# Sigmoid attention and a bilinear FFN: x passed through memory in 512-token blocks, twelve plain pairs, w1 and w2 decoded in twelve pieces

## The chip, the core and the metric

The kernel runs on one NeuronCore of a Trainium2 chip. The metric is the device time of one execution in microseconds (us); of several executions the median is taken.

## The reference

Eight batches of twelve heads, 448 tokens, head size 64. Attention has a sigmoid in place of a softmax; its output is the input x of a bilinear feed-forward net on 3584 tokens:

```
scores = q @ k.T / 8 - log(448)
x      = concat_heads(sigmoid(scores) @ v)          # 3584 x 768
out    = ((x @ w1) * (x @ w2)) @ w3 @ w_out         # 768 -> 1024 -> 1024 -> 768
```

All arrays are float32, except that the host hands over w1, w2, w3 and w_out as 64-bit words of float64 values, which the kernel decodes to float32 itself.

## The kernel before

**Precision by splitting.** A float32 operand is split into a high part rounded to float32r and the rest as a low part (`split`, L66 casts, L67 subtracts). A product of two such operands is then three float32r matmuls: high by high, high by low, low by high. "Plain" pairs of heads skip this: their scores (L196) and their products with v (L248) are float32 matmuls.

**Attention in slots.** Two heads make a pair; 8 batches of 6 pairs are 48 pairs. The keys of a pair fall into four chunks (128, 128, 128 and 64 keys, NC = 4); one chunk is a slot, so there are 192. In a slot the program writes the score products (`scores`, or `short_scores` for the 64-key chunk of a split pair, L225), the sigmoids on ScalarE (L180; split pairs take two of them, and VectorE makes the low part al, L217), the decode and split steps that fall due, a dozen products of the filler, and then the av products (L255 or L248) of the slot before. Before the change the first 9 pairs (PLAIN) are plain. `split_pair` makes qs, kh, kl, ks of the next pair: VectorE casts qs and kh and subtracts (L158, L159, L66), POOL makes kl (L67) and ks (L165). After the last chunk, `combine` writes x of the pair as xh and xl into SBUF; two sets of six such tiles (px0, px1) serve even and odd batches.

**The up products as filler.** `up(b)` is a generator of 288 matmuls for one batch: 8 fc by 2 weights by 6 kc by 3, each of 448 columns (L318). Between slots `take` draws 12 of them (`ups`). The up products of batch b - 1 run while batch b is in attention, from its slot 2 on; those of batch 7 run after attention. Each fc ends with a copy of the w1 product (a_sb, L326), a multiply (g, L329) and a store to memory at once (L330).

**Decoding weights.** A job loads words (L74), takes the magnitude on ScalarE (`magnitude`, Abs, L79), does six VectorE operations (`decode`, L86, L91, L94, L98, L99, L102), and is split into w high (ScalarE, L66) and w low (VectorE, L67) some slots later. w1 and w2 take 16 jobs of 768 elements a partition, the first eight from slot 1 on, three slots apart, the others from slot 25 on; w3 takes 16 jobs of 512 during attention, which go back to memory; w_out is decoded after attention in 16 halves.

**After attention** come the last up products, w3 times w_out (L508), and the output products of 512 columns (L524), in seven blocks of TB = 512 tokens, for which g is loaded from memory.

**Order.** Until slot PLAIN x NC - 2 the order of TensorE, SP (which issues the DMAs), ScalarE and POOL is as written; after it that of TensorE and SP only, and a scheduler orders the others. VectorE's order is the scheduler's from the start. At that slot the pool pp of early words gives its memory to the tiles of the split pairs (pf).

Of the kernel before, what the change touches and what calls it, by code (L numbers as in the profile page):

```python
# [25 lines left out]
def sigmoid_attention_bilinear_ffn(  # L26
# [16 lines left out]
    nc = tc.nc  # L43
# [12 lines left out]
    PLAIN = 9  # L56
# [5 lines left out]
    w3_dram = dram.tile([NF, P, NF, P], F32, name="w3_dram")  # L62
    g_dram = dram.tile([NF, P, NT], F32, name="g_dram")
# [5 lines left out]
    def load_words(src, pool=None):  # L69
        if pool is None:  # L70
            raw = pd.tile([P, NK, P, 2], U32, name="raw", bufs=1)[:, :src.shape[1]]
# [5 lines left out]
    def magnitude(raw, early=False):  # L77
        f = (pp if early else pd).tile([P, *raw.shape[1:-1]], F32, name="f", bufs=3 if early else 2)
        nc.scalar.activation(f, raw[..., 1].bitcast(F32), AF.Abs, scale=HW_SCALE)  # L79
        return f  # L80
# [26 lines left out]
    px1 = phase_x.enter_context(tc.tile_pool(name="px1", bufs=NK, side="left"))  # L107
    pm = phase_x.enter_context(tc.tile_pool(name="pm", bufs=2, side="left"))
# [3 lines left out]
    px = (px0, px1)  # L112
# [147 lines left out]
    def combine(b, accs):  # L260
        xh = px[b % 2].tile([P, S], F32R, name="xh")
        xl = px[b % 2].tile([P, S], F32R, name="xl")
        if len(accs) == 1:
            split(xh, xl, accs[0][:, :S], nc.scalar.copy, nc.vector)
            return xh, xl
        t = pm.tile([P, S], F32, name="t", bufs=1)
        add_halves(t, [acc[:, :S] for acc in accs])
        split(xh, xl, t, nc.scalar.copy, nc.vector)
        return xh, xl
# [19 lines left out]
    def load_job(i):  # L289
        _, _, cs, src = jobs[i]  # L290
        raws[i] = load_words(src[:, cs], pp) if i < EARLY else load_words(src[:, cs])

    def decode_job(i):
        if i + 2 < EARLY:
            load_job(i + 2)
        for k in (i, i + 1):
            if k not in fs and k in raws:
                fs[k] = magnitude(raws[k], k < EARLY)
        f = decode(raws.pop(i), fs[i])
        if EARLY <= i + 1 < len(starts):  # L300
            load_job(i + 1)
        n, at, cs, _ = jobs[i]
        if n == 3:
            nc.sync.dma_start(out=w3_dram[at, :, cs], in_=f)

    def split_job(i):
        n, at, cs, _ = jobs[i]
        split(wh[n][:, at, cs], wl[n][:, at, cs], fs.pop(i), nc.scalar.copy, nc.vector)

    def up(b, xs, banks):  # L310

        for fc in range(NF):
            for n in (1, 2):
                acc = ps.tile([P, 512], F32, name="up", tag=next(banks), bufs=2)
                for kc in range(NK):
                    xh, xl = xs[kc]
                    for m, (w, x) in enumerate(((wh[n], xh), (wh[n], xl), (wl[n], xh))):
                        nc.tensor.matmul(  # L318
                            acc[:, :S], w[:, fc, kc], x,
                            start=(kc == 0 and m == 0), stop=(kc == NK - 1 and m == 2),  # L320
                        )
                        if (kc, m) != (NK - 1, 2):
                            yield
                if n == 1:
                    a_sb = pm.tile([P, S], F32, name="a_sb", bufs=1)
                    nc.scalar.copy(out=a_sb, in_=acc[:, :S])  # L326
                    yield
            g = pm.tile([P, S], F32, name="g", bufs=1)
# [234 lines left out]
```

## Time and profile before

| what | value |
|---|---|
| median of 3 runs | 1082.26 us (1080.23 to 1083.45) |
| profiled execution, its time | 1081.56 us |
| its span, first to last instruction | 1079.5 us |
| granted TensorE clock, mean | 0.998 |
| busy share of the span | TensorE 99%, VectorE 66%, ScalarE 52%, POOL 18% |
| DMA | 129.15 MB, mean 120 GB/s |

PE is TensorE, PEld its weight loads, DVE is VectorE, ACT ScalarE, SPq the queue of the engine that issues DMAs. A matmul's listed duration (some 370 ns at 448 columns) holds its way through the array, in which the next one already runs; what a product costs the engine is the distance between two starts. A bracket behind a row of the timeline says how long the engine was idle before it and what ended that.

### The profile page before, as it was taken

Reading aid. Unit: us, or ns where it says so; the run is one execution under the profiler, and the core shown is the slowest. Engines: PE = TensorE matmul, PEld = TensorE weight load, DVE = VectorE, ACT = ScalarE, POOL = GpSimd, SP = SyncE. Lnnn points to the kernel's source line nnn. Section 1 sums busy time; section 2 is a strip of 40 time slices with the busy share of each in tenths; the row PEclk is TensorE's granted clock in tenths of the full one; section 3 lists DMA queues with packets and bytes.
Section 4 is the critical chain, followed back from the end, with each engine's and each line's share of the span. In section 5 each row is a group of like instructions: output and inputs, shape, how many; then the busy total and the mean of one; then the engine's idle time right before and its main releaser. Section 6 shows DMA issues by size and latency. Waiting matters only on the chain.

```text
span 1079.5 us, 14155 instructions
## 1 busy us (share of the span) xinstructions
PE 1067.9 (99%) x5094; PEld 915.1 (85%) x5094; DVE 714.1 (66%) x1074; ACT 563.4 (52%) x789; POOL 190.1 (18%) x277
## 2 busy tenths in 40 slices
PE   8999899999999999999999999999999999999998
PEld 3256799999999999999999989999999888888886
DVE  5997978888878878888887877649862133223321
ACT  5855666776776677767767766653342011101100
POOL 0002432232233323232332224200000000000000
PEclk9999999999999999999999999999999999999999
DMA  8755434443543535344452543225471032233211
GB/s 257 231 166 146 103 95 122 124 132 104 140 118 103 141 107 135 112 131 115 116 154 79 135 122 92 68 75 180 137 243 39 20 127 93 84 127 127 88 49 49
DMA packets 100693, 129.15 MB, mean 120 GB/s; under 512 B 8016, under 2 KB 82960, under 8 KB 100624
## 3 DMA queue, kind: packets, MB, share of 16 engines
q1 hardware_dynamic: 100624, 128.25, 40.6%
q8 instruction: 40, 0.66, 0.3%
q14 instruction: 29, 0.24, 0.1%
HBM read 98.34 MB, written 29.88 MB: 119 GB/s over the span
## 4 chain that ended last, share of the span: by engine, by line
PE 94%; DVE 2%; DMA 1%; ACT 1%; issue 1%; SPq 0%; ACTq 0%
PE up L318 42%; PE up L524 21%; PE av L255 10%; PE sp L199 9%; PE up L508 6%; PE sp L196 2%; PE av L248 2%; PE sp L225 1%; DMA raw<-w 1%; DVE f L102 0%; ACT f L79 0%; DVE w L67 0%; DVE raw L99 0%; DVE f L94 0%; ACT ap L180 0%
## 5 line engine op out<-in xcount | busy, mean ns | idle before, releaser
L318 PE MATMUL up<-xh,w 128*128 128x448 f32 x1536 | 467.2, 368 | 0.0
L318 PEld LDWEIGHTS up<-xh,w 128*128 128x128 f32 x1536 | 288.8, 188 | 31.6 <-issue 5.9
L318 PE MATMUL up<-xl,w 128*128 128x448 f32 x768 | 281.2, 366 | 0.0
L524 PE MATMUL up<-w 128*128 128x512 f32 x1008 | 228.7, 389 | 0.0
L524 PEld LDWEIGHTS up<-w 128*128 128x128 f32 x1008 | 189.2, 188 | 39.2
L180 ACT ACTIVATE ah<-sp,bias 128x896 fp32r<-128x896 f32 x117 | 117.6, 1005 | 114.3 <-PE sp L199 113.5
L217 DVE TENSOR_TENSOR al<-sp,ah 128x896 fp32r<-128x896 f32 x117 | 127.5, 1090 | 50.0 <-ACT sp L180 49.0
L67 POOL TENSOR_TENSOR kl<-kk,kh 128x896 fp32r<-128x896 f32 x39 | 89.5, 2294 | 402.5 <-DVE kh L66 380.3
L318 PEld LDWEIGHTS up<-xl,w 128*128 128x128 f32 x768 | 144.4, 188 | 12.5
L534 DVE COPY o_sb<-up 128x512 f32<-128x512 f32 x42 | 29.0, 691 | 161.0 <-PE up L524 161.0
L66 ACT CAST w<-graw 128x1024 fp32r<-128x1024 f32 x28 | 29.4, 1056 | 175.9 <-PE up L524 170.5
L180 ACT ACTIVATE sp<-sp,bias 128x896 f32<-128x896 f32 x117 | 113.6, 971 | 0.0
L255 PE MATMUL av<-ah,vs 128*128 128x448 f32 x312 | 102.4, 368 | 3.8 <-DVE ah L239 2.7
L255 PE MATMUL av<-al,vs 128*128 128x448 f32 x234 | 86.1, 368 | 0.4 <-DVE al L217 0.4
L199 PE MATMUL sp<-qs,kh 128*128 128x448 f32 x234 | 86.3, 369 | 0.0
L67 POOL TENSOR_TENSOR vs<-vv,vs 128x256 fp32r<-128x256 f32 x78 | 68.2, 885 | 102.8 <-DVE vs L66 95.0
L199 PE MATMUL sp<-qs,kl 128*128 128x448 f32 x234 | 86.3, 369 | 0.0
L239 DVE TENSOR_TENSOR ah<-st,ah 64x448 fp32r<-64x448 f32 x78 | 59.3, 760 | 18.7 <-ACT st L180 16.8
L255 PEld LDWEIGHTS av<-ah,vs 128*128 128x128 f32 x312 | 58.5, 188 | 10.3 <-DVE ah L239 2.8
L79 ACT ACTIVATE f<-raw 128x768 f32<-128x768 f32 (+2 forms) x48 | 34.4, 716 | 48.3 <-DMA raw<-w_out 17.7
L186 ACT COPY t<-av 64x448 f32<-64x448 f32 x78 | 41.3, 529 | 32.3 <-PE av L255 31.2
L180 ACT ACTIVATE ah<-st,bias 64x448 fp32r<-64x448 f32 x78 | 52.2, 670 | 4.0 <-DVE st L187 2.0
(57 smaller groups left out, 1243.4 us busy)
## 6 DMA issues: line engine op xcount, KB each, us to landing
qq<-qT SPq DMA_DIRECT2D x78, 224.0 KB, 3.9
kk<-kT SPq DMA_DIRECT2D x78, 224.0 KB, 4.5
g_dram<-g SPq DMA_DIRECT2D x64, 224.0 KB, 2.0
graw<-g_dram SPq DMA_DIRECT2D x14, 1024.0 KB, 5.3
raw<-w SPq DMA_DIRECT2D x16, 768.0 KB, 5.3
out<-o_sb SPq DMA_DIRECT2D x42, 256.0 KB, 2.0
vv<-vL SPq DMA_DIRECT2D x48, 192.0 KB, 2.8
raw<-w3T SPq DMA_DIRECT2D x16, 512.0 KB, 4.1
```

What stands on the lines that cost most here:

```text
L66: hi_engine(out=dst_hi, in_=src)
L67: lo_engine.tensor_tensor(out=dst_lo, in0=src, in1=dst_hi, op=ALU.subtract)
L79: nc.scalar.activation(f, raw[..., 1].bitcast(F32), AF.Abs, scale=HW_SCALE)
L180: nc.scalar.activation(dst, src, AF.Sigmoid, bias=bias[:n], scale=scale)
L186: nc.scalar.copy(out=dst[rows], in_=src[j][others])
L199: nc.tensor.matmul(sp[:, j], k[:, j, at:at + n], qs[:, j], start=m == 0, stop=m == 1)
L217: nc.vector.tensor_tensor(out=al, in0=sp, in1=ah, op=ALU.subtract)
L239: nc.vector.tensor_tensor(out=a[others, j], in0=t[rows], in1=a[rows, j], op=ALU.subtract)
L255: nc.tensor.matmul(accs[j][:, :S], v[:, c, j].rearrange("p u d -> p (u d)"), a[:, j], start=first and m == 0, stop=last and m == len(ops) - 1,
L318: nc.tensor.matmul(acc[:, :S], w[:, fc, kc], x, start=(kc == 0 and m == 0), stop=(kc == NK - 1 and m == 2),)
L508: nc.tensor.matmul(acc[:, :NM], a[:, jc], w[:, jc, ms], start=(jc == 0 and m == 0), stop=(jc == NF - 1 and m == 2),)
L524: nc.tensor.matmul(acc[:, :TB], w[:, fc, ms], g[:, at, fc % NH], start=(fc == 0 and m == 0), stop=(fc == NF - 1 and m == 2),)
```

## The change

Three things are changed together.

- **x goes through memory in blocks.** The up products are made for seven blocks of 512 tokens in place of eight batches of 448, two batches behind attention: block c's 288 products, now of 512 columns, start in batch c + 2 (block 0 in the first pair's slot 1, the others in the second pair's slot 0), at 11 a slot up to slot 75 and 12 after it. The high and low parts of block 0 stay in SBUF; everything behind token 512 is stored to x_dram two slots after its pair is done, and loaded again block by block: kc 0 and 1 at the start of fc 6 of the block before, kc 2 to 5 one by one as the last fc, whose order is changed for that, frees a tile (eight px tiles). The g store waits until the middle of the next fc; block 6 runs after attention.
- **Twelve plain pairs in place of nine**: batches 0 and 1 are plain, batches 2 to 7 split.
- **w1 and w2 decoded in twelve jobs** of two kc by 512 columns, 1024 elements a partition, all in the plain stretch, 3.7 slots apart, the last due to be split in slot 44. A w3 job loads its words in the slot that decodes them (before: two slots ahead), and its store is issued five slots later.

The diff, cut to its core:

```diff
-    PLAIN = 9
+    TB = 512
+    PLAIN = 2 * NPAIR
+    x_dram = dram.tile([NK, P, 2, NT], F32, name="x_dram")
-    px1 = phase_x.enter_context(tc.tile_pool(name="px1", bufs=NK, side="left"))
+    px = phase_x.enter_context(tc.tile_pool(name="px", bufs=NK + 2, side="left"))
-    px0 = phase_a.enter_context(tc.tile_pool(name="px0", bufs=NK, side="right"))
...
-        split(xh, xl, accs[0][:, :S], nc.scalar.copy, nc.vector)
+        at = b * S
+        n = min(max(TB - at, 0), S)
+        if n:
+            if b == 0:
+                blocks[0][kc] = px.tile([P, 2, TB], F32R, name="x")
+            x = blocks[0][kc][:, :, at:at + n]
+            split(x[:, 0], x[:, 1], src[:, :n], nc.scalar.copy, nc.vector)
+        if n < S:
+            x = pa.tile([P, 2, S], F32R, name="xs")[:, :, n:]
+            split(x[:, 0], x[:, 1], src[:, n:], nc.scalar.copy, nc.vector)
+            stores.append((due, x_dram[kc, :, :, at + n:at + S], x.bitcast(F32), (kc, at + S)))
+
+    def load_block(c, kc):
+        blocks[c][kc] = px.tile([P, 2, TB], F32R, name="x")
+        nc.sync.dma_start(
+            out=blocks[c][kc].bitcast(F32), in_=x_dram[kc, :, :, c * TB:(c + 1) * TB]
+        )
...
-        (n, fc, slice(0, NK), words(w, slice(fc * P, (fc + 1) * P)))
-        for fc in range(NF) for n, w in ((1, w1), (2, w2))
+        (n, slice(fc, fc + NF // 2), slice(kc, kc + 2), words(w, slice(fc * P, (fc + NF // 2) * P)))
+        for fc in range(0, NF, NF // 2) for kc in range(0, NK, 2) for n, w in ((1, w1), (2, w2))
...
         if i + 2 < EARLY:
             load_job(i + 2)
+        elif i >= EARLY:
+            load_job(i)
...
-        if EARLY <= i + 1 < len(starts):
-            load_job(i + 1)
-            nc.sync.dma_start(out=w3_dram[at, :, cs], in_=f)
+            stores.append((starts[i] + 5, w3_dram[at, :, cs], f, None))
...
+            if fc == NF - 2 and following:
+                for kc in range(2):
+                    load_block(following, kc)
+            passes = [(1, kc) for kc in range(NK)] + [(2, kc) for kc in range(NK)]
+            if fc == NF - 1:
+                passes.sort(key=lambda s: s[1] + 3.5 * s[0])
...
+                    nc.tensor.matmul(
+                        accs[n], w[:, fc, kc], xs[kc][:, i],
+                        start=(kc == 0 and m == 0), stop=(kc == NK - 1 and m == 2),
+                    )
                     yield
+                if (fc, n) == (NF - 1, 2) and following and kc + 2 < NK:
+                    load_block(following, kc + 2)
+                if (n, kc) == (1, NK - 1):
+                    a_sb = pm.tile([P, TB], F32, name="a_sb")
+                    nc.scalar.copy(out=a_sb, in_=accs[1])
+                    if ready:
+                        store(*ready)
...
-    first = NPAIR * NC
-    starts = [1 + 3 * i for i in range(8)] + [first + 1 + 4 * i // 3 for i in range(8)]
-    later = [(2 * NPAIR + 2 * i) * NC + 1 for i in range(2 * NF)]
+    EARLY = 2 * NK
+    starts = [1 + 37 * i // 10 for i in range(EARLY)]
+    starts += [(2 * NPAIR + 2 * i) * NC + 1 for i in range(2 * NF)]
+    steps = {s + 3: [(split_job, i)] for i, s in enumerate(starts[:EARLY])}
...
-                xs[b].append(combine(b, accs.pop(p)))
+                combine(*pairs[p], accs.pop(p), slot + 2)
...
+            store_due(slot)
             prepare(p, i)
...
-            if b > 0 and (hp, i) == (0, 2):
+            if b > 1 and (hp, i) == ((0, 1) if b == 2 else (1, 0)):
                 take(filler, 10 ** 6)
-                filler = up(b - 1, xs[b - 1], itertools.repeat("up"))
-            take(filler, ups)
+                filler = up(b - 2, itertools.repeat("up"))
+            take(filler, ups if slot >= (3 * NPAIR + 1) * NC else ups - 1)
...
     attend_due(slot)
+    store_due(10 ** 6)
     take(filler, 10 ** 6)
...
-    filler = up(B - 1, xs[B - 1], banks)
+    filler = up(NT // TB - 1, banks)
```

## Rows read from the trace of the kernel before

**Rows 1.** The profile page: part 1, busy time, share and count of TensorE and the others; part 4, the chain that ended last, by line.

```profile
PE 1067.9 (99%) x5094; PEld 915.1 (85%) x5094; DVE 714.1 (66%) x1074; ACT 563.4 (52%) x789; POOL 190.1 (18%) x277
...
PE up L318 42%; PE up L524 21%; PE av L255 10%; PE sp L199 9%; PE up L508 6%; PE sp L196 2%; PE av L248 2%; PE sp L225 1%; DMA raw<-w 1%; DVE f L102 0%; ACT f L79 0%; DVE w L67 0%; DVE raw L99 0%; DVE f L94 0%; ACT ap L180 0%
```

**Rows 2.** The chain that ended last, in order of time, from the end of attention on: start, length, what, and how many instructions in a row.

```profile
716.81 63.30 PE up L318 x312
...
847.19 228.54 PE up L524 x1008
```

**Rows 3.** The same chain in the attention stretch of split pairs (one pair's pieces, and an up piece from later on).

```profile
402.44 1.24 PE av L255 x6
...
404.50 2.44 PE up L318 x12
406.94 0.82 PE av L255 x4
407.76 0.41 PE sp L225 x2
...
454.74 2.46 PE up L318 x12
```

**Rows 4.** The same chain in the plain stretch, slot 7, and the up products of slot 26, the first that has any.

```profile
22.07 0.95 PE sp L196 x4
23.02 0.90 PE av L248 x4
...
58.55 2.66 PE up L318 x12
```

**Rows 5.** Busy time of each engine by stretch: from:to, its length, then busy us and count for PE, PEld, DVE, ACT, POOL, then the granted clock, the DMA engines' busy share and GB/s.

```profile
5.00:13.00 8.00, 8.00 (x33) 3.41 (x33) 1.99 (x3) 2.70 (x4) 0.00 (x0) 1.00 1.06 336
...
21.00:58.50 37.50, 37.01 (x161) 9.44 (x161) 36.70 (x52) 31.24 (x40) 0.00 (x0) 1.00 0.77 235
...
122.00:126.00 4.00, 4.00 (x14) 3.56 (x13) 3.42 (x5) 1.59 (x2) 2.85 (x3) 0.57 0.00 0
126.00:700.00 574.00, 572.94 (x2802) 525.60 (x2801) 464.13 (x698) 409.45 (x582) 175.28 (x259) 1.00 0.43 117
```

**Rows 6.** The timeline of the first slots: ScalarE's second Abs, its first w cast, and the two av groups that waited.

```profile
12.98 0.90 ACT L79 ACTIVATE f<-raw 128x768 f32<-128x768 f32 x1 [2.73 <-DMA raw<-w]
...
14.83 0.97 PE L248 MATMUL av<-ap,vv 128*64 128x448 f32 x4 [1.12 <-ACT ap L180]
...
18.06 0.83 ACT L66 CAST w<-f 128x768 fp32r<-128x768 f32 x1 [0.18 <-DVE f L102]
...
21.10 0.97 PE L248 MATMUL av<-ap,vv 64*64 64x448 f32 x4 [0.68 <-ACT ap L180]
```

**Rows 7.** VectorE's timeline: the first operation (L86) of four decode jobs, the last split of one (L67), and operations of both kinds at 768 and at 512 elements.

```profile
21.27 0.55 DVE L86 TENSOR_SCALAR raw<-raw 128x768 uint32<-128x768 uint32 x1
...
33.07 0.56 DVE L86 TENSOR_SCALAR raw<-raw 128x768 uint32<-128x768 uint32 x1
...
34.13 0.96 DVE L94 SCALAR_TENSOR_TENSOR f<-f,raw 128x768 uint32<-128x768 uint32 x1
...
38.01 0.95 DVE L67 TENSOR_TENSOR w<-f,w 128x768 fp32r<-128x768 f32 x1
38.88 0.56 DVE L86 TENSOR_SCALAR raw<-raw 128x768 uint32<-128x768 uint32 x1
...
44.27 0.56 DVE L86 TENSOR_SCALAR raw<-raw 128x768 uint32<-128x768 uint32 x1
...
627.85 0.43 DVE L86 TENSOR_SCALAR raw<-raw 128x512 uint32<-128x512 uint32 x1 [2.79 <-ACT f L79]
...
632.75 0.69 DVE L94 SCALAR_TENSOR_TENSOR f<-f,raw 128x512 uint32<-128x512 uint32 x1
```

**Rows 8.** Where plain pairs give way to split ones: timeline of VectorE, POOL and TensorE, and the pieces of av and up of the chain behind them.

```profile
95.29 1.09 DVE L159 TENSOR_TENSOR qs<-qq,qs 64x896 fp32r<-64x896 f32 x1
...
115.37 3.00 POOL L67 TENSOR_TENSOR kl<-kk,kh 128x896 fp32r<-128x896 f32 x1 [11.34 <-DVE kh L66]
...
116.44 2.74 DVE L67 TENSOR_TENSOR w<-f,w 128x768 fp32r<-128x768 f32 x1
...
117.08 0.37 PE L318 MATMUL up<-xh,w 128*128 128x448 f32 x1
...
119.89 0.47 PE L255 MATMUL av<-ah,vs 128*128 128x448 f32 x1 [2.43 <-DVE ah L239]
...
121.66 1.22 PE av L255 x3
...
124.37 2.98 PE up L318 x12
```

**Rows 9.** Who waited for whom between 130 and 700 us (total us, times, longest), for SP's queue and for ScalarE.

```profile
SPq L330 <- DVE g L329: 251.2, 37, 8.9
...
ACT f L79 <- DMA raw<-w3T: 5.4, 5, 2.7
```

**Rows 10.** DMA: bytes moved by slice of the span (page, part 2), and issues by tile: KB each, median us to landing.

```profile
GB/s 257 231 166 146 103 95 122 124 132 104 140 118 103 141 107 135 112 131 115 116 154 79 135 122 92 68 75 180 137 243 39 20 127 93 84 127 127 88 49 49
...
raw<-w3T SPq DMA_DIRECT2D x16, 512.0 KB, 4.1
...
w<-w_dram SPq DMA_DIRECT2D x8, 512.0 KB, 5.1
```

More of the change, by code (lines that the diff above doesn't have):

```diff
@@ L67, in split, with load_words @@
         lo_engine.tensor_tensor(out=dst_lo, in0=src, in1=dst_hi, op=ALU.subtract)
[L69 to L71 removed]
+    def load_words(src, pool):
+        if pool is pd:
+            raw = pd.tile([P, NF // 2, P, 2], U32, name="raw", bufs=1)
         else:
@@ L75, in load_words, with magnitude @@
         return raw
-    def magnitude(raw, early=False):
-        f = (pp if early else pd).tile([P, *raw.shape[1:-1]], F32, name="f", bufs=3 if early else 2)
+    def magnitude(raw, pool=pd):
+        f = pool.tile([P, *raw.shape[1:-1]], F32, name="f", bufs=3 if pool is not pd else 2)
         nc.scalar.activation(f, raw[..., 1].bitcast(F32), AF.Abs, scale=HW_SCALE)
@@ L258, in attend, with combine, store_due @@
                 )
-    def combine(b, accs):
-        xh = px[b % 2].tile([P, S], F32R, name="xh")
-        xl = px[b % 2].tile([P, S], F32R, name="xl")
+    blocks = {c: {} for c in range(NT // TB)}
+    stores, stored = [], {}
+    def combine(b, kc, accs, due):
         if len(accs) == 1:
-            split(xh, xl, accs[0][:, :S], nc.scalar.copy, nc.vector)
[L265 to L269, printed above, removed]
+            src = accs[0][:, :S]
+        else:
+            src = pa.tile([P, S], F32, name="t", bufs=1)
+            add_halves(src, [acc[:, :S] for acc in accs])
+        at = b * S
[9 more added lines that the diff above has]
+            stores.append((due, x_dram[kc, :, :, at + n:at + S], x.bitcast(F32), (kc, at + S)))
+    def store_due(slot):
+        for entry in [e for e in stores if e[0] <= slot]:
+            stores.remove(entry)
+            if entry[3]:
+                kc, end = entry[3]
+                stored[kc] = end
+            nc.sync.dma_start(out=entry[1], in_=entry[2])
+    def load_block(c, kc):
+        assert stored[kc] >= (c + 1) * TB
+        blocks[c][kc] = px.tile([P, 2, TB], F32R, name="x")
+        nc.sync.dma_start(
+            out=blocks[c][kc].bitcast(F32), in_=x_dram[kc, :, :, c * TB:(c + 1) * TB]
+        )
     wh, wl = {}, {}
@@ L306, in split_job @@
     def split_job(i):
         n, at, cs, _ = jobs[i]
-        split(wh[n][:, at, cs], wl[n][:, at, cs], fs.pop(i), nc.scalar.copy, nc.vector)
-    def up(b, xs, banks):
-        for fc in range(NF):
[L313 to L326, printed above, removed]
-                    yield
-            g = pm.tile([P, S], F32, name="g", bufs=1)
-            nc.vector.tensor_tensor(out=g, in0=acc[:, :S], in1=a_sb, op=ALU.mult)
-            nc.sync.dma_start(out=g_dram[fc, :, b * S:(b + 1) * S], in_=g)
-            yield
@@ new lines, in split_job, with up, store @@
+        hi, lo = (w[n][:, at, cs].rearrange("p f k c -> p k f c") for w in (wh, wl))
+        split(hi, lo, fs.pop(i).rearrange("p k (f c) -> p k f c", c=P), nc.scalar.copy, nc.vector)
+    def up(c, banks):
+        xs, following = blocks[c], c + 1 if c + 1 in blocks else None
+        ready = None
+        def store(fc, g):
+            nc.sync.dma_start(out=g_dram[fc, :, c * TB:(c + 1) * TB], in_=g)
+        for fc in range(NF):
+            if fc == NF - 2 and following:
[4 more added lines that the diff above has]
+                passes.sort(key=lambda s: s[1] + 3.5 * s[0])
+            accs = {}
+            for n, kc in passes:
+                if kc == 0:
+                    accs[n] = ps.tile([P, TB], F32, name="up", tag=next(banks), bufs=2)
+                for m, (w, i) in enumerate(((wh[n], 0), (wh[n], 1), (wl[n], 0))):
+                    nc.tensor.matmul(
+                        accs[n], w[:, fc, kc], xs[kc][:, i],
+                        start=(kc == 0 and m == 0), stop=(kc == NK - 1 and m == 2),
+                    )
+                    yield
+                if (fc, n) == (NF - 1, 2) and following and kc + 2 < NK:
[5 more added lines that the diff above has]
+                        store(*ready)
+            g = pm.tile([P, TB], F32, name="g")
+            nc.vector.tensor_tensor(out=g, in0=accs[2], in1=a_sb, op=ALU.mult)
+            ready = fc, g
+        store(*ready)
@@ L372, in sigmoid_attention_bilinear_ffn @@
     splits, vs = {0: split_pair(0 < PLAIN, *qks.pop(0))}, {0: split_v(0 < PLAIN, vvs.pop(0))}
-    xs = {b: [] for b in range(B)}
     filler = iter(())
```

25 lines of the change are left out of this document (8 added, 17 removed).

## Prediction, made before the result was known

> **What bounds the kernel now.** I read the profile page first: TensorE is busy 99% of the span, and of the chain that ended last the up products (L318) alone are 42%, the output products (L524) 21% [rows 1]. Busy time of overlapping matmuls overstates the work, so I priced matmuls by their spacing in the chain in order of time: 312 up products take 63.30 us after attention and 1008 products of 512 columns take 228.54 us in the last stage [rows 2]; twelve up products take 2.44 to 2.46 us between split pairs, and 6 + 4 + 2 attention products 1.24 + 0.82 + 0.41 = 2.47 us [rows 3]. A plain slot is 0.95 us of sp and 0.90 us of av, 1.85 us [rows 4]. The stage table then says who stands next to TensorE: VectorE is 98% busy in the plain stretch (36.70 of 37.50 us) and 81% in the attention stretch behind it [rows 5]. A run of such products without holes would be shorter than the span; the holes sit at the start [rows 6] and where plain pairs give way to split ones [rows 8]. A difference under 0.3% (3.2 us) can't be told from none here.
>
> **The change part by part**, against the profiled span of 1079.5 us.
>
> *Wider up products.* Before, 8 batches x 288 = 2304 products of 448 columns: 312 in 63.30 us; ten plain slots (26 to 35) carry twelve each at 2.66 us per twelve [rows 4], 26.6 us; 1872 at 2.45/12 = 0.204 us, 382.3 us. Sum 472.2 us. After, 7 blocks x 288 = 2016 of 512 columns. L524 has that shape at 228.54/1008 = 0.2267 us [rows 2], so 457.1 us. Between attention products a 448-column product is 1.3 ns dearer than in the quiet stage (0.2042 against 0.2029); 1680 of the new ones lie there, 2.2 us more. Sum 459.3: **-12.9 us**. The Trainium skill, page "TensorE: Matmul & The Clock Gate", section "Back-to-back issue gap", gives N/2.4 + 2.5 ns for a warm product, 189.2 ns at 448 columns and 215.8 at 512: the trace disagrees with both sizes (204 and 227), and by that rule the regrouping would save 0.8 us.
>
> *Three pairs from split to plain.* A split pair has 28 products at 2.47/12 = 0.206 us [rows 3]; three fewer: **-17.3 us**. Twelve more plain slots at 1.85 us each [rows 4]: **+22.2 us**. So this part alone loses 4.9 us; it buys room, because batches 0 and 1 no longer carry up products.
>
> *The old hand-over stall.* Between 117.08 and 121.66 us four products start where 0.82 us would do: 3.8 us of waiting for ah and al, behind a split of w that took VectorE 2.74 us while POOL held kl for 3.00 [rows 8]. Then the granted clock is 0.57 of 2.4 GHz in the next 4 us [rows 5], that is, mostly the 1.2 GHz level, after TensorE had stood idle; three av products take 1.22, the four sp up to 124.37 then 1.49 and twelve up 2.98 us in place of 0.61, 0.82 and 2.46, 1.8 us more [rows 8]. After the change the last w split is due at slot 44, ahead of the first split pair (slot 48), so both go: **-5.6 us**.
>
> *The bigger decode pieces at the start.* Two first transfers grow from 768 to 1024 KB; 0.52 MB more at the 336 GB/s of that stage [rows 5] is 1.6 us, and the Abs on them gets some 0.3 us longer. ScalarE keeps its order: the second Abs waits for its words [rows 6], and slot 2's sigmoid comes behind it, so TensorE waits 1.8 us longer than its 1.12. Then the w cast of job 0 waits for VectorE's sixth operation (18.06); those operations fall 4.1 us behind the second Abs now, 5.2 by size, and cast and Abs grow 0.25 each: 1.6 us more. **+3.4 us**. Bounds: 0 (the wait is covered) and 7 (twice).
>
> *VectorE in the plain stretch.* One job of 768 takes 5.39 us without an x part and 5.81 with it; operations of 512 elements take 0.43 (three of a job are of that kind) and 0.69 us (four) where 768 take 0.56 and 0.96 [rows 7]. So 1024 costs 3 x 0.13 + 4 x 0.27 = 1.47 us more: 6.86, with its share of x parts 7.36, every 3.7 slots (6.85 us of TensorE). VectorE falls behind. Job 2 starts at 21.27 now; with 1.9 us of later words and a quarter more work on 7.35 us it starts at 25.2, job 11 at 25.2 + 9 x 7.36 = 91.4. Its sixth operation ends 4.94 us after the start today, 6.3 by size: 97.7. ScalarE's cast behind that takes 1.0, then slot 45's sigmoid is ready at 99.7; TensorE, at slot 7 at 25.4, wants it at 25.4 + 39 x 1.85 + 0.95 = 98.5. **+1.2 us**. Bounds 0 and 6 (3.7 slots against 7.36 us, twelve times).
>
> *The new hand-over.* No up product fills slot 48. Behind the last lo part (99.9) come qs, its difference and kh on VectorE, 2.2 us by their spacing, then kl on POOL: 3.00 where it ran against the w split [rows 8], and I take 2.4 without it: 104.5. TensorE reaches slot 48 at 102.5 and does one kh product before it needs kl: **+1.8 us**. Bounds 0 and 5.6, the old stall come back.
>
> *x through memory.* 42 stores of up to 448 KB and 36 loads of 512 KB join SP's queue, 64 g stores become 56, words come in 12 transfers for 16. Their issue (about 0.5 us each) is hidden: SP spends 251 us waiting for g [rows 9], and that wait shrinks, as g and w3 stores are issued later than now. What counts is the lead of the four late loads at each boundary: every one is issued at least 21 products before its first use, 4.8 us of products plus some two slots' attention products, 8.0 us in all. The nearest rows land 512 KB in 4.1 and 5.1 us [rows 10]. Four loads are 2.1 MB; beside the 117 GB/s that the stretch moves, 336 - 117 leaves 219 GB/s, 9.6 us from the first issue, and with attention products between, the last is needed 13 us after it. In SP's order such a load stands behind qq and kk of the pair after next, which go out as soon as POOL's ks has read the old ones, and ahead of the next v; one that waits for its tile holds that v for less than a slot, and v is wanted two slots later. So nothing at the five boundaries inside attention. The last one lies behind attention, with 8.2 us: up to 2.4 late, I take half. **+1.2 us**. Bounds 0 and 15 (third rival). If this cover goes, TensorE stands, for the next block's products are all that is left on it there.
>
> *At no cost.* Extra x splits, wider a_sb and g copies lie on ScalarE and VectorE in slots that get longer (12 x 0.2267 for 2.45); VectorE is at 81% there. The w3T words are now loaded in the slot that decodes them; ScalarE waited 5.4 us for them in five places, behind an SP queue that stood on g [rows 9], and TensorE was idle for only 1.06 of 574 us there [rows 5]. I leave that as it is; range 0 to 5. The w_out decode starts later behind the block loads, but has 76 us of products (336 x 0.2267) for today's 63.
>
> Sum: -12.9 - 17.3 + 22.2 - 5.6 + 3.4 + 1.2 + 1.8 + 1.2 = -6.0, span 1073.5. The execution took 1081.56 us, 2.06 over its span, and the median lies 0.70 above it: **1076.3 us**.
>
> **The rivals.**
> - *The waits are covered* (0.15). The 7.6 us of new waits are sums of late arrivals, and VectorE's order is free, so it may bring job 0 and kh forward. For: in the plain stretch TensorE idles only 0.49 us beside a VectorE at 98% [rows 5]. Against: the start waits of 1.12 and 0.68 us exist already [rows 6]. Time 1068.7.
> - *The hand-over stall stays* (0.20). kl on POOL and VectorE's two-tensor operations slow each other, as the 2.74 us row shows, the clock falls again, and -5.6 does not come: 1081.9, no measurable change. For: the first pair's kl, ks and vs on POOL remain. Against: the decode that competed is gone.
> - *The boundary loads come late* (0.11), slower than before. At a boundary the same queue carries qq and kk of a later pair (0.9 MB), w3T words (0.5), an x store, v and g: 4.0 MB with the four loads. It decides once these take over 13 us, below 308 GB/s; the best slice of the profile page moves 257 [rows 10]. At that, 15.6 us: 2.6 late at five boundaries and 2.4 at the last, 15.4 instead of 1.2: 1090.5. For: 336 GB/s was seen only at the start. Against: not all 4.0 MB fall into the same 13 us; v and w3T are issued a slot earlier.
> - *Columns alone have a price* (0.04), slower. If an up product costs 0.204/448 per column whatever its width, 512 take 0.2335 us, 2016 take 470.6 us and the first term shrinks from 12.9 to 1.6: 1087.6. Against: L524's 0.2267. The skill's rule named above is of this kind: its fixed part is only 2.5 ns.
>
> **How the numbers follow.** The forecast has 0.50 and reaches from 1071 to 1081; one part in sixteen of it lies above 1079.0 (0.3% below the median), as does most of the hand-over rival. Faster 0.15 + 0.47 = 0.62, same 0.03 + 0.18 = 0.21, slower 0.15 + 0.02 = 0.17. The range 1066 to 1087 takes in the first two rivals and the bounds of the start and of the hand-over, and leaves out the late loads and the column price.
>
> **What would show it.** Up products in shape 128x512, 2016 of them, twelve in about 2.72 us of the chain; 48 plain slots at 1.85; split pairs at 5.8 us of products. Idle rows of TensorE at slots 2 and 5 some 3 us longer in sum, one near 98 to 105 us; first up product near 106. No clock drop behind it. At each boundary no wait of TensorE for x but the last. Wrong would be: w casts of ScalarE waiting for VectorE many times in the plain stretch, up products over 0.230 us, or TensorE waiting for the x transfers at every boundary.

## The result: slower by 0.8%, where 0.5% faster was forecast

The changed kernel takes 1089.77 us (median of six runs, 1088.81 to 1093.24), the kernel before 1081.8 beside it: ratio 1.0083, 95% interval 1.0063 to 1.0103. The forecast was 1076.3, its range 1066 to 1087. The profiled execution of after has a span of 1087.9 us, 14.4 more than the 1073.5 of the sum. Three executions among the later runs (of e4_plain12, f1_casts_noclamp and i1_late_bare) took 1269 to 2142 us and count in no ratio below; that of i1_late_bare is the profiled one, so none of its waits is read.

The page of after: part 1, which answers to the first row of [rows 1], and the two groups of the up products.

```profile
PE 1067.2 (98%) x4818; PEld 850.3 (78%) x4818; DVE 682.2 (63%) x1002; ACT 543.8 (50%) x752; POOL 170.9 (16%) x256
...
L360 PE MATMUL up<-x,w 128*128 128x512 f32 x2016 | 485.4, 391 | 0.2
L360 PEld LDWEIGHTS up<-x,w 128*128 128x128 f32 x2016 | 378.3, 188 | 77.6 <-DMA x<-x_dram 1.6
```

The regrouping was done as described: 2016 products of 512 columns. Their weight loads wait for x only 1.6 us in all, in four places (the products themselves 0.2), so x through memory is not the loss. The stage table of after, with the columns of [rows 5], says where it is.

```profile
24.00:64.00 40.00, 39.53 (x175) 10.12 (x172) 39.41 (x44) 33.39 (x38) 0.00 (x0) 1.00 0.77 243
64.00:70.00 6.00, 5.17 (x24) 1.19 (x20) 5.93 (x8) 2.85 (x4) 0.00 (x0) 1.00 0.56 197
70.00:74.00 4.00, 0.25 (x2) 0.25 (x4) 3.93 (x7) 1.68 (x3) 0.00 (x0) 0.92 0.00 0
74.00:80.00 6.00, 6.00 (x16) 1.34 (x14) 5.46 (x7) 3.57 (x4) 0.00 (x0) 0.50 0.78 215
80.00:113.00 33.00, 29.25 (x128) 7.24 (x124) 24.59 (x29) 22.96 (x30) 2.94 (x2) 1.00 0.57 169
113.00:150.00 37.00, 35.02 (x155) 27.63 (x154) 31.40 (x44) 23.90 (x35) 13.68 (x21) 1.00 0.65 169
150.00:712.00 562.00, 561.11 (x2540) 476.01 (x2539) 423.99 (x635) 376.59 (x533) 154.07 (x231) 1.00 0.58 166
```

From 150 us on TensorE has hardly a hole (0.9 of 562 us). Those that the sum did not have lie between 64 and 150: TensorE stands for almost all of 70 to 74 us, while VectorE is 98% busy there, and then runs six microseconds at a granted clock of 0.50, the 1.2 GHz level. TensorE's rows with idle time, in the timeline of after from 62 us to slot 48 and in the first split pairs:

```profile
65.80 0.97 PE L249 MATMUL av<-ap,vv 128*64 128x448 f32 x4 [0.36 <-ACT ap L181]
73.75 1.76 PE L249 MATMUL av<-ap,vv 64*64 64x448 f32 x4 [4.23 <-ACT ap L181]
92.53 0.97 PE L249 MATMUL av<-ap,vv 64*64 64x448 f32 x4 [0.97 <-ACT ap L181]
101.56 0.97 PE L249 MATMUL av<-ap,vv 64*64 64x448 f32 x4 [1.52 <-ACT ap L181]
110.24 0.97 PE L249 MATMUL av<-ap,vv 64*64 64x448 f32 x4 [1.25 <-ACT ap L181]
...
134.83 0.44 PE L256 MATMUL av<-ah,vs 128*128 128x448 f32 x1 [0.43 <-DVE t L188]
140.41 0.44 PE L200 MATMUL sp<-qs,kh 128*128 128x448 f32 x1 [0.97 <-DVE st L188]
145.04 0.47 PE L256 MATMUL av<-al,vs 128*128 128x448 f32 x1 [0.39 <-DVE al L218]
```

It waits for sigmoids (ap), but ScalarE is not busy then. ScalarE's and VectorE's rows around 72 us say what it stood on:

```profile
66.82 0.21 ACT L69 CAST x<-av 128x64 fp32r<-128x64 f32 x1 [0.18 <-PE av L249]
72.32 0.48 ACT L69 CAST xs<-av 128x384 fp32r<-128x384 f32 x1 [5.29 <-DVE x L70]
72.70 1.00 ACT L181 ACTIVATE ap<-sp,bias 64x896 f32<-64x896 f32 x1
```

```profile
66.60 1.23 DVE L105 TENSOR_TENSOR f<-f,raw 128x1024 f32<-128x1024 f32 x1
67.74 1.22 DVE L70 TENSOR_TENSOR w<-f,w 128x1024 fp32r<-128x1024 f32 x1
...
72.07 0.22 DVE L70 TENSOR_TENSOR x<-av,x 128x64 fp32r<-128x64 f32 x1
```

In batch 1 the x of a pair has two parts, 64 tokens for block 0 and 384 for memory. ScalarE's order is as written: cast, then the second cast, which waits for VectorE's 0.22 us subtraction between them; that stands behind six operations of the decode and the split of w, of which the first (66.60) was already running. The sigmoid waits behind the second cast, and TensorE waits for the sigmoid. The chain in order of time then shows the price of the low clock (compare 0.95 and 0.90 in [rows 4]):

```profile
73.75 1.76 PE av L249 x4
75.51 1.79 PE sp L197 x4
77.30 1.69 PE av L249 x4
78.99 1.57 PE sp L197 x4
```

These are 6.81 us for what takes 3.70: 3.1 us. Behind 80 us VectorE is no longer full (24.59 of 33), for the held ScalarE now hands it its work late. Of VectorE's waits between 80 and 113 us:

```profile
DVE w L70 <- ACT w L69: 6.1, 4, 3.7
```

**Where the 14.4 us are.** The first product that needs kl should have started at 104.5; it does at 113.5:

```profile
L200 PE MATMUL sp<-qs,kh x216: 362/368/440, 113.2 to 707.2; 128*128 128x448 f32 x108
L200 PE MATMUL sp<-qs,kl x216: 358/367/370, 113.5 to 707.4; 128*128 128x448 f32 x108
```

That is 9.0 of the 14.4. The other 5.4 lie behind it: 1.8 are the three waits listed after 130 us, 2.0 are the up products, dearer than priced, and 1.6 are what is left of smaller gaps. The price, from the chain at 402 and 730 us of after:

```profile
402.01 2.75 PE up L360 x12
...
729.96 59.16 PE up L360 x261
```

2.75/12 = 0.2292 us between split pairs, where I had 0.2280 (1680 x 0.0012 = 2.0 us), and 0.2267 in the quiet stage, as priced.

### The profile page after: what moved, and what is told of

It reads as the page before. It is cut to its first block, busy times and chain, and to the rows that moved or that the text cites. A ratio compares the mean times of both kernels' runs of the same rounds, so it can differ in the third digit from the quotient of the medians.

```text
span 1087.9 us, 13564 instructions
## 1 busy us (share of the span) xinstructions
PE 1067.2 (98%) x4818; PEld 850.3 (78%) x4818; DVE 682.2 (63%) x1002; ACT 543.8 (50%) x752; POOL 170.9 (16%) x256
## 4 chain that ended last, share of the span: by engine, by line
PE 86%; DVE 7%; DMA 3%; issue 2%; ACT 2%; SPq 0%; ACTq 0%; DVEq 0%
PE up L360 40%; PE up L560 21%; PE av L256 9%; PE sp L200 8%; PE up L544 6%; PE sp L226 1%; DVE f L97 1%; DVE raw L102 1%; DMA x<-x_dram 1%; DMA raw<-w 1%; PE av L249 1%; PE sp L197 1%; DVE w L70 1%; DVE raw L89 1%; ACT ap L181 1%
## 5 line engine op out<-in xcount | busy, mean ns | idle before, releaser
L360 PE MATMUL up<-x,w 128*128 128x512 f32 x2016 | 485.4, 391 | 0.2
L360 PEld LDWEIGHTS up<-x,w 128*128 128x128 f32 x2016 | 378.3, 188 | 77.6 <-DMA x<-x_dram 1.6
L181 ACT ACTIVATE ah<-sp,bias 128x896 fp32r<-128x896 f32 x108 | 108.5, 1004 | 132.3 <-PE sp L200 132.1
L218 DVE TENSOR_TENSOR al<-sp,ah 128x896 fp32r<-128x896 f32 x108 | 117.8, 1091 | 82.6 <-ACT sp L181 80.7
L70 POOL TENSOR_TENSOR kl<-kk,kh 128x896 fp32r<-128x896 f32 x36 | 76.8, 2133 | 362.2 <-DVE kh L69 215.2
L181 ACT ACTIVATE sp<-sp,bias 128x896 f32<-128x896 f32 x108 | 104.7, 970 | 0.0
L240 DVE TENSOR_TENSOR ah<-st,ah 64x448 fp32r<-64x448 f32 x72 | 48.0, 667 | 22.3 <-ACT st L181 20.6
L249 PE MATMUL av<-ap,vv 128*64 128x448 f32 (+1 forms) x192 | 49.0, 590 | 12.6 <-ACT ap L181 10.9
L181 ACT ACTIVATE ap<-sp,bias 128x896 f32<-128x896 f32 (+1 forms) x48 | 47.8, 1005 | 19.4 <-PE sp L197 19.4
L197 PE MATMUL sp<-qp 64*128 64x448 f32 (+1 forms) x192 | 50.6, 606 | 0.0
```

The lines of the kernel that those rows point to most:

```text
L70: lo_engine.tensor_tensor(out=dst_lo, in0=src, in1=dst_hi, op=ALU.subtract)
L181: nc.scalar.activation(dst, src, AF.Sigmoid, bias=bias[:n], scale=scale)
L197: nc.tensor.matmul(sp[:, j], kh[rows, at:at + n], qs[rows], start=True, stop=True)
L218: nc.vector.tensor_tensor(out=al, in0=sp, in1=ah, op=ALU.subtract)
L240: nc.vector.tensor_tensor(out=a[others, j], in0=t[rows], in1=a[rows, j], op=ALU.subtract)
L249: nc.tensor.matmul(accs[0][cols, :S], v[:ops[0].shape[0], c, cols], ops[0][:, j], start=first, stop=last,)
```

## The experiments

Ratios are to the kernel before in runs on the same chip. "Order theory": the wait at 72 us is made by the written order of casts and goes when that is changed. "Load theory": VectorE has, by my prices (12 x 6.86 and some 6 for x parts), 88 us of work for 89 us of bare plain slots (48 x 1.85); whatever is reordered, its lag comes out at the next place that needs VectorE.

### e1_casts: ScalarE's two casts of x first

```diff
-            split(x[:, 0], x[:, 1], src[:, :n], nc.scalar.copy, nc.vector)
...
-            split(x[:, 0], x[:, 1], src[:, n:], nc.scalar.copy, nc.vector)
+            nc.scalar.copy(out=x[:, 0], in_=src[:, :n])
+            nc.scalar.copy(out=xs[:, 0], in_=src[:, n:])
...
+        if n:
+            nc.vector.tensor_tensor(out=x[:, 1], in0=src[:, :n], in1=x[:, 0], op=ALU.subtract)
```

> The two ScalarE casts of a pair's x (64 tokens for block 0, 384 for memory) are issued ahead of both VectorE subtractions; nothing else changes. Order theory (in batch 1 ScalarE's second cast waits for VectorE's first subtraction, which stands deep in VectorE's queue): the five waits of xs, 11.5 us of ScalarE and 8.0 us of TensorE, are gone, and so is the clock drop at 73 us, worth 3.4 us: 1078 to 1080 us. Load theory (VectorE has more work than 3.7 plain slots hold, wherever the wait shows): the waits move to the w casts, and the time stays at 1086 or more.

1088.29 us, ratio 1.0051 (1.0031 to 1.0071). The xs waits are gone and slot 48 starts at 106.5 instead of 113.2, yet most of it is given back. TensorE's rows with idle time behind 80 us in this kernel:

```profile
83.21 0.97 PE L249 MATMUL av<-ap,vv 128*64 128x448 f32 x4 [2.13 <-ACT ap L181]
91.78 0.97 PE L249 MATMUL av<-ap,vv 128*64 128x448 f32 x4 [1.14 <-ACT ap L181]
106.47 0.44 PE L200 MATMUL sp<-qs,kh 128*128 128x448 f32 x1 [0.84 <-issue]
108.36 0.47 PE L200 MATMUL sp<-qs,kl 128*128 128x448 f32 x1 [1.45 <-POOL kl L70]
123.73 0.47 PE L256 MATMUL av<-ah,vs 128*128 128x448 f32 x1 [1.04 <-DVE ah L240]
125.19 0.64 PE L256 MATMUL av<-ah,vs 128*128 128x448 f32 x2 [1.00 <-DVE ah L240]
```

TensorE is earlier at the hand-over than VectorE and POOL are: the stall that I had forecast there, and that the late TensorE of after had hidden, comes up. At 83 us the chain leads back through ScalarE, which waited 2.65 us for words, to SP's queue: the load of these words stood there behind a store of x, and that store waited for VectorE's subtraction xs. SP's waits from 66 to 84 us, and the load in the chain:

```profile
SPq L293 <- DVE xs L284: 9.2, 2, 5.4
...
74.27 6.78 DMA raw<-w
```

The order theory fell as an explanation of the time, though not of the lag: slot 48 starts 6.7 us earlier.

### e2_start: job 1's Abs in its own slot

```diff
-        for k in (i, i + 1):
+        for k in (i, i + 1) if i else (i,):
```

> The Abs of job 1 is taken in job 1's own slot and no longer ahead of slot 2's sigmoid; batch 1 is left as it is. By the start term of the prediction TensorE reaches slot 7 some 2.5 us earlier (22.7 for 25.2 us) and the clock does not fall at 18.7 us. Order theory: the batch 1 waits stay as long as they are, so the gain stays: 1086 to 1088 us. Load theory: VectorE gets job 1 later and must make it up, so its later waits grow by what the start gains: 1089 to 1090 us.

1090.57 us, ratio 1.0074 (1.0047 to 1.0100), with an interval that overlaps after's. The granted clock is 1.00 from 13 to 24 us, where after has 0.84, and nothing is gained: waits of 1.90 and 2.30 us come at 21.9 and 29.8 instead.

### e3_noclamp: one VectorE operation less in each decode

```diff
-        nc.vector.tensor_scalar(out=f, in0=f, scalar1=HW_MIN, scalar2=HW_MAX, op0=ALU.max, op1=ALU.min)
```

> Leaves out one of the six decode operations (the clamp of the magnitude to the smallest and largest float32), in every decode: 12 x 0.61 us less for VectorE in the plain stretch, a job with its x part 6.75 us against 6.85 us of slots; the order of the x casts is as in the changed kernel. Load theory: VectorE keeps up, the waits for it go and with them the clock drop: 1078 to 1080 us. Order theory: the second cast still stands behind the first subtraction, which stands behind several decode operations, so half of the 8.0 us stays: 1084 to 1086 us.

1083.47 us, ratio 1.0005 (0.9994 to 1.0017). Twelve operations of 0.69 us, 8.3 us of VectorE's work in the plain stretch, are worth some 8 us of the time (1.0083 against 1.0005; 6.3 by the medians). It lies between the two theories' numbers. Slot 48 starts at 108.4; no clock drop is left behind the start, and TensorE still waits often for sigmoids, but never long:

```profile
PE av L248 <- ACT ap L180: 8.8, 9, 2.1
```

### e4_plain12: the kernel before, with twelve plain pairs and nothing else

```diff
-    PLAIN = 9
+    PLAIN = 12
```

> The kernel before with twelve plain pairs in place of nine and nothing else: up products of 448 columns as before, one batch behind, sixteen decode jobs of 768. By the prediction's prices three pairs cost 22.2 - 17.3 = 4.9 us more; the hand-over comes after the decode, so its stall of 5.6 us should go: 1080 to 1083 us with both, 1086 to 1088 us if the stall stays. A rival price for the pairs (plain slots dearer with up products between them) would show as more than 1090 us.

1082.99 us, ratio 1.0003 (0.9993 to 1.0014). Here the decode has the same twelve plain pairs, but batch 1's carry up products. Stretches of this kernel:

```profile
44.00:64.00 20.00, 20.00 (x89) 7.71 (x88) 19.62 (x29) 15.49 (x19) 0.00 (x0) 1.00 0.75 226
64.00:80.00 16.00, 16.00 (x73) 8.87 (x71) 15.71 (x23) 7.04 (x10) 0.00 (x0) 1.00 0.55 167
```

Up to 64 us VectorE is as full as in after, and neither kernel loses 0.5 us of TensorE there behind 24 us. From 64 to 80 VectorE is still 98% busy, but TensorE has no hole where after loses 4.6 us: the up products, which begin in batch 1, cover it. Between 98 and 130 us VectorE is busy for only 6.41 us, and slot 48 is only reached at 155.7 us, without a wait. The exchange of three pairs costs nothing, as priced (-17.3 + 22.2 - 5.6 = -0.7).

### f1_casts_noclamp: both of these edits

> Both earlier edits in one: ScalarE's two casts of a pair's x ahead of VectorE's two subtractions, and the clamp of every decode left out (VectorE does one operation less per piece; the weights that overflow are then wrong). Alone the first gave -1.5 us and the second -6.3 us against the changed kernel. Load theory (what costs is VectorE's lag, wherever it surfaces): the two add at most, 1082 us, because the casts only move the wait. Load and order together (with VectorE no longer full, the waits of xs casts are the whole of what is left, 8.8 us of TensorE's idle time in the run without the clamp): 1075 us, and no clock drop after slot 5.

1083.27 us, ratio 1.0009 (0.9999 to 1.0019): nothing beyond the clamp alone. Slot 48 now starts at 102.5, the very time that the sum had for TensorE, where the clamp alone had 108.4; the hand-over takes back what is won:

```profile
104.27 0.47 PE L199 MATMUL sp<-qs,kl 128*128 128x448 f32 x1 [1.28 <-POOL kl L70]
110.66 0.47 PE L255 MATMUL av<-al,vs 128*128 128x448 f32 x1 [1.28 <-DVE al L217]
...
120.73 0.65 PE L255 MATMUL av<-ah,vs 128*128 128x448 f32 x2 [0.99 <-DVE ah L239]
```

### f2_casts_pool: casts first, w low of w1 and w2 on POOL

```diff
-        split(hi, lo, fs.pop(i).rearrange("p k (f c) -> p k f c", c=P), nc.scalar.copy, nc.vector)
+        split(hi, lo, fs.pop(i).rearrange("p k (f c) -> p k f c", c=P), nc.scalar.copy, nc.gpsimd)
```

> Casts first, and the low part of w1 and w2 pieces subtracted on POOL instead of VectorE: 12 operations of 1.1 to 1.4 us leave VectorE's plain stretch, some 14 us of its 88. The computation is whole. Load theory: more relief than without the clamp, so 1076 to 1080 us. Rival (POOL and VectorE slow each other, as in the rows where a split of 2.7 us stood beside kl): POOL's operation takes 3 us or more, VectorE's others beside it get longer by as much as it saved, and the time stays at 1086 to 1090 us.

1096.45 us, ratio 1.0131 (1.0116 to 1.0146): the rival, and worse than its 1086 to 1090. Groups from 24 to 98 us, two of this kernel, then VectorE's in e1_casts:

```profile
L97 DVE SCALAR_TENSOR_TENSOR f<-f,raw 128x1024 uint32<-128x1024 uint32 x9 | 25.9, 2875 | 0.3
L70 POOL TENSOR_TENSOR w<-f,w 128x1024 fp32r<-128x1024 f32 x10 | 25.1, 2512 | 73.8 <-ACT w L69 73.8
```

```profile
L97 DVE SCALAR_TENSOR_TENSOR f<-f,raw 128x1024 uint32<-128x1024 uint32 x10 | 12.4, 1235 | 0.3
```

POOL's 2.51 us stand beside VectorE's operation of two inputs, which takes 2.88 instead of 1.24: 1.64 us lost on it for the 1.22 that VectorE was spared. The Trainium skill, page "SBUF — State Buffer", section "SBUF: two separate sides", says that GpSimd (POOL) and a VectorE operation with two inputs from SBUF share a port pair that one holds for its whole instruction while the other blocks. These rows agree: where L97 starts 0.08 and 0.62 us behind POOL's subtraction, at 52.47 and 44.70 us, it takes 3.36 and 3.26 us.

### f3_casts_qk: casts first, qq and kk of the first split pair two slots earlier

```diff
-        if i == 0 and change:
+        if i == 0 and n == PLAIN + 1:
             qks[n] = load_pair(*pairs[n])
+        if (p, i) == (PLAIN - 2, 2):
+            qks[PLAIN] = load_pair(*pairs[PLAIN])
```

> Casts first, and qq and kk of the first split pair loaded at slot 42 instead of 44, with two more buffers for them. Lead theory (leads that are counted in slots shrank with the slots; kh waited 0.96 us for kk, TensorE 1.45 us for kl at the hand-over): the hand-over loses 1.5 to 2.5 us of waits and perhaps its clock drop of 1.7 us, 1084.5 to 1086 us against 1088.3 with casts first alone. Load theory: VectorE reaches qs and kh no earlier, the waits for ah and al stay, 1087.5 to 1089 us.

1085.81 us, ratio 1.0038 (1.0026 to 1.0049), 0.13% below e1_casts with overlapping intervals. The time is in the lead theory's range, but the wait for kl stays (1.45 us at 107.85), and the run does not test the lead: in SP's order the loads still stand behind the same store of x, and qq goes out at 96.93, right behind it, as in e1_casts (store 96.92, qq 97.54). So kh still waits for kk:

```profile
96.32 0.56 SPq L293 DMA_DIRECT2D x_dram<-xs  x1
...
104.11 0.63 DVE L69 CAST kh<-kk 128x896 fp32r<-128x896 f32 x1 [1.03 <-DMA kk<-kT]
```

That store waits for VectorE's subtraction xs; VectorE's lag thus reaches kl by way of SP's queue.

### e7_pieces: casts first, sixteen pieces of 768

```diff
+        (n, slice(fc, fc + 1), slice(0, NK), words(w, slice(fc * P, (fc + 1) * P)))
+        for fc in range(NF) for n, w in ((1, w1), (2, w2))
...
+    starts = [1 + 27 * i // 10 for i in range(EARLY)]
```

> Casts first, and w1 and w2 decoded in sixteen pieces of 768 elements, as before the change, started every 2.7 slots instead of every 3.7. VectorE's work is then 16 x 5.39 = 86.2 us beside x parts, against 12 x 6.86 = 82.3 with pieces of 1024. Load theory: no better than casts first alone (1088.3), rather 2 to 4 us worse, 1088 to 1092 us, with a start that is 3 us shorter. Burst theory (the large piece is the cost: words 8 us late, casts held for 7 us at a time): 1080 to 1084 us.

1088.56 us, ratio 1.0055 (1.0038 to 1.0072), e1_casts again. The size of the pieces, the edit whose start I priced at +3.4, is not the cause. e4_plain12 has the same pieces and the same plain pairs, and up products over batch 1; the two also differ in when the second eight pieces start and in x's way through memory, so this pair alone doesn't isolate the cover.

### g1_late2, g2_late4: the last pieces behind slot 48

```diff
+    BIG = 10
+    jobs = jobs[:BIG] + [
+        (n, at, slice(k, k + 1), src) for n, at, cs, src in jobs[BIG:] for k in range(cs.start, cs.stop)
+    ]
...
+    starts = [1 + 43 * i // 10 for i in range(EARLY)] + [50, 53, 56, 59]
```

This is g2_late4, which has the casts first and f3's earlier loads too; g1_late2 has the casts first, BIG = 11, a step of 40 and the late starts 51 and 55.

> Casts first, and the last of the twelve pieces (w2, upper half, two of its rows) taken out of the plain stretch: eleven pieces of 1024 elements start every 4.0 slots, the twelfth comes as two pieces of 512 at slots 51 and 55, ahead of block 0's products that use it (slot 62 on); w3 is decoded 8 slots later. The computation is whole. VectorE's plain stretch falls from 12 x 6.86 + 6 = 88 us to 81, beside 89 us of TensorE's plain slots. Load theory: the lag inside the stretch goes, slot 48 is reached at 103 us instead of 106.5, the hand-over keeps its waits of some 6 us: 1082 to 1084 us. Rival (the waits follow from the order in which each engine takes its work, however much of it there is): 1086 to 1089 us.

> As the kernel before it in this call, but the last two pieces (w1 and w2) are taken out, as four of 512 elements at slots 50, 53, 56 and 59; ten pieces of 1024 start every 4.3 slots, qq and kk of the first split pair are loaded at slot 42, and w3 is decoded 15 slots later. VectorE's plain stretch falls to 75 of 89 us. Load theory: neither the plain stretch nor the hand-over waits for VectorE by more than 3 us together, and the time comes to where my sum had it, 1074 to 1079 us. Rival (the work only moves to where al and ah need VectorE, 8 us of decode in slots that have 19% of it free): TensorE waits for al and ah in slots 50 to 62, 1083 to 1087 us.

1082.27 us, ratio 1.0003 (0.9992 to 1.0014), and 1082.16, ratio 0.9991 (0.9979 to 1.0004). With the computation whole and 8% and 15% less of VectorE's work in the plain stretch (81 and 75 us for 88, by my prices), the lag is gone: slot 48 starts at 101.8 and 100.6. TensorE's rows with idle time in g2_late4, from 12 to 150 us, without two of 0.2 us around 106:

```profile
17.09 1.03 PE L249 MATMUL av<-ap,vv 128*64 128x448 f32 x4 [2.30 <-ACT ap L181]
...
123.83 0.44 PE L256 MATMUL av<-ah,vs 128*128 128x448 f32 x1 [0.62 <-DVE t L188]
131.40 0.47 PE L256 MATMUL av<-ah,vs 128*128 128x448 f32 x1 [0.28 <-DVE ah L240]
132.87 0.65 PE L256 MATMUL av<-ah,vs 128*128 128x448 f32 x2 [1.00 <-DVE ah L240]
146.56 0.44 PE L200 MATMUL sp<-qs,kh 128*128 128x448 f32 x1 [1.15 <-DVE st L188]
```

Between 18 us and slot 48 there is no wait, and none for kl at the hand-over. What is left are waits for VectorE where the late pieces run. g1 has them earlier, at the hand-over (1.58 us for qs at 101.77, 1.40 for kl at 103.61). The load theory held for the plain stretch and for g1's time (1082 to 1084); its number for g2 (1074 to 1079) did not.

### h1_late4_noclamp, h2_late4_kh

```diff
-        split(kh, kl, kk, nc.vector.tensor_copy, nc.gpsimd)
+        split(kh, kl, kk, nc.scalar.copy, nc.gpsimd)
```

This is h2's edit on g2_late4; h1 has the clamp's line taken out instead.

> As with four late pieces (1082.2 us beside 1082.0 of before), but the clamp is left out of every decode, so VectorE does one operation less in each of 30 pieces and in w_out's (weights that overflow are then wrong). In the run with the clamp the plain stretch was bare from slot 7 and the hand-over had no stall, yet the attention stretch behind it took 7 us more than 594, TensorE waiting for ah, t and st where the four late pieces ran. Load theory: these waits shrink by 2 to 4 us, 1078 to 1080 us. Rival (the waits are the fixed latency of ScalarE to VectorE to TensorE at a pair's short chunk, whatever VectorE's load): no change, 1081.5 to 1082.5.

> As with four late pieces, but the high part of k (kh) is cast on ScalarE instead of VectorE in every split pair: 0.62 us a pair leave VectorE, some 0.9 us a pair come to ScalarE, which is busy 67% there. The computation is whole. Load theory: the waits behind the late pieces shrink and nothing else is late, 1078 to 1081 us. Rival (ScalarE takes kh ahead of the sigmoids that TensorE waits for, and kl on POOL starts later): 1082 to 1086 us.

h1: 1082.56 us, ratio 1.0004 (0.9994 to 1.0014), no gain on g2, as the rival had it. h2: 1079.73 us, ratio 0.9976 (0.9965 to 0.9987), the best of the versions that compute the whole. That a clamp less buys nothing there while a cast less does, I can't explain from the rows.

### i1 to i4: what is left behind slot 48

```diff
-        f = decode(raws.pop(i), fs[i])
+        f = fs[i] if EARLY <= i < LATE else decode(raws[i], fs[i])
+        del raws[i]
```

This is i1, on h2. i2 is h2 with late starts at 49, 53, 57 and 60; i3 is h2 with eleven pieces every 4.0 slots and two late ones at 51 and 56; i4 has h2's edit of kh alone, on the changed kernel.

> As the best version so far (four late pieces, kh on ScalarE, 0.9976 of before), but VectorE's six decode operations are left out of the four late pieces (their words, Abs, cast and low part stay; these weights are then wrong): 4 x 3.4 us of VectorE's work between slots 50 and 59 gone. If the waits for t, st and ah between 120 and 160 us are VectorE's queue behind the late pieces, TensorE gains 3 to 5 us: 1075 to 1077 us, ratio 0.993 to 0.995. If they are fixed latencies of a pair's short chunk: no gain, ratio 0.997 to 0.998.

> As the best version so far, but the four late pieces start at slots 49, 53, 57 and 60, one a pair instead of 4 in 10 slots. If VectorE's queue makes the waits: each pair has 17 us and some 16 us of VectorE's work, so the waits halve, ratio 0.995 to 0.997. If they are fixed: 0.997 to 0.998; if the first pieces collide with the hand-over (slots 48 to 50): 0.998 to 1.000.

> Casts first, eleven pieces of 1024 every 4.0 slots and two late ones of 512 at slots 51 and 56, qq and kk at slot 42, kh on ScalarE, w3 12 slots later. VectorE's plain stretch 81 of 89 us. If late pieces are the cost behind slot 48: 2 us less than with four, ratio 0.995 to 0.997. If the hand-over is: its waits of 5 us come back, as with two late pieces and kh on VectorE (1.0003), 0.999 to 1.001.

> The changed kernel with one edit: kh is cast on ScalarE in every split pair. The plain stretch is as in the changed kernel, so its 9 us of lag stay. If VectorE's queue is what the first split pairs wait for: 1.5 to 3 us less than 1.0083 of before, 1.0055 to 1.007. If not: 1.008 to 1.0095.

i1: 1076.9 us, ratio 0.9953 (0.9939 to 0.9968); the 13.6 us (my estimate, 4 x 3.4) of VectorE's decode in the late pieces cost some 0.23%, or 2.5 us, beside h2; the two intervals touch. i2: 1081.02, ratio 0.9980 (0.9967 to 0.9992): spreading them changes nothing. i3: 1082.51, ratio 0.9997 (0.9985 to 1.0010): with eleven pieces in the plain stretch one wait of 3.34 us at 103.5 is back, and the low clock behind it. i4: 1092.87, ratio 1.0089 (1.0065 to 1.0113): kh on ScalarE alone brings no measurable gain while the lag is there.

## Why the prediction was wrong

- **VectorE in the plain stretch (+1.2, bounds 0 and 6): the step that failed.** From slot 7 (25.21) to slot 48 (113.20) TensorE takes 88.0 us for 41 slots at 1.85: 12.1 us over, where I had 1.2 and at most 6. Its idle time there sums to 8.3 us (the five rows from 65.80 to 110.24), and the low clock adds 3.1. I had followed VectorE's queue to its last piece only, and asked when the last sigmoid is late. The sum of VectorE's lag was nearly right: in e1_casts its row for the sixth operation of the last job starts at 96.75 and lasts 1.2, where I had 97.7 for its end. But ScalarE asks VectorE for something in every piece and every pair, in written order, and SP's queue holds loads behind stores of x that wait for VectorE, so the lag of the moment is passed on several times, not once at the end. Slot 48's start says what it takes to lose the lag: 113.2 in after, 106.5 with the casts first, 108.4 with a clamp less, 102.5 with both. The written order and the load carry about half of it each. I had the two-part split under "at no cost", in slots that get longer; for batch 1 they do not.
- **The cover that went.** The general form: [rows 5] show VectorE as full (36.70 of 37.50 us) before the change, without harm, since plain slots with up products follow [rows 4]. I costed 22.2 us for more bare slots, and saw that they must carry twelve pieces, but checked the balance (7.36 us of VectorE per 6.85 of TensorE) as a small drift. e4_plain12, where the products cover a VectorE that is 98% busy, and g1_late2 and g2_late4, where less work and the casts first leave no wait, show that this balance is the loss: 9.0 of the 14.4 us.
- **The new hand-over (+1.8) was not paid in after**, since TensorE came late to it itself; as soon as it came in time (e1_casts, f1, f3) it was, with 1.3 to 1.5 us for kl and 1.2 to 2.0 us for ah behind it, and low clocks besides. This is the second step that was mis-sized, hidden by the first: the sum left 971.0 us from slot 48's start to the end; after takes 974.7, e3_noclamp 972.0, but f1, which is there on time, 979.8, and g2_late4 979.7. With the plain stretch mended the kernel therefore comes to the time of before and not to the forecast, and what the sum won from the old stall (5.6) is largely lost again at the new one.
- **Wider up products (-12.9)**: 1680 x 0.2292 + 336 x 0.2267 = 461.2 us, so -11.0. Right in kind, 1.9 too good: the premium between attention products is 2.5 ns, not 1.3.
- **The start (+3.4)**: slot 7 at 25.21, forecast 25.4. Right in size. e2_start shows that it is not worth mending by itself.
- **Pairs and old stall (-17.3, +22.2, -5.6)**: right in the kernel before, by e4_plain12, where slot 48 comes long after the decode.
- **x through memory (+1.2)**: right in size; 1.6 us, though in four places of 0.2 to 0.5 us and not at the last boundary alone. The rival of late boundary loads and the column price are refuted by these rows (1.6 us at PEld, 0.2292 us).
- The sign of the result came from a rival I had not listed: a side engine that keeps its work and loses its cover. One of my signs of being wrong named it ("w casts of ScalarE waiting for VectorE many times in the plain stretch"), but I gave it no chance.

Open: the first four split pairs keep some 3 us of waits, most of them for t and ah, even in the best version (h2, 130 to 160 us); i1 puts 2.5 us on the late pieces. Why g2_late4 takes 5.0 us more than after from slot 48 to the end, more than its listed waits, isn't settled. A version whose plain pairs carry block 0's products was not tried: block 0 needs 64 tokens of batch 1.

## What to carry to other kernels

Before moving filler work off a stretch, ask what that stretch was covering: add up the side engine's whole work against the new, shorter stretch. Here 88 us for 89 lagged, and 81 for 89 did not once the casts were first. Count every place where another engine or a DMA queue waits for the side engine in order, not just the last. An edit that removes one such wait shows little in the time, since the lag comes out at the next; here it took less work as well. A load that is issued earlier in the program gains nothing while its queue stands on a store before it (f3).

## What the runs showed of the hardware

- The length of TensorE's idle time alone did not tell whether the clock fell. 4.23 us in after were followed by six microseconds at 0.50; in e1_casts 2.13 us at 83 us were not, but the 1.45 us for kl, 0.84 us of idle time before it, were (0.61 from 108 to 112 us). The stages of e1_casts, with the columns of [rows 5]:

```profile
83.00:88.00 5.00, 4.79 (x22) 1.32 (x24) 4.90 (x7) 4.46 (x7) 0.00 (x0) 1.00 0.92 241
108.00:112.00 4.00, 3.64 (x10) 1.64 (x11) 0.70 (x2) 2.40 (x4) 2.52 (x7) 0.61 0.54 134
```

- POOL's subtraction of 1024 elements more than doubled the two-input operation of VectorE that fell beside it (L97 in f2_casts_pool, 2875 against 1235 ns), so that VectorE lost more than it was spared; L102, of the same size but not beside it, stayed at 1227 against 1231.
- Which of the two paid followed from which started first. In e1_casts VectorE's difference of qs starts at 105.28 and takes 1.09 us, POOL's kl starts at 105.47 and takes 2.84; in after kl starts first, at 110.06, and takes 2.08, and the difference, at 110.34, takes 2.76. I had 2.4 for kl.
